# A three-stage kernel (pooled attention and two feed-forward layers): the whole program in written order, weight combination in single steps over three stages

## The chip, the cores and the metric

One core of a Trainium2 chip. The metric is device time in microseconds (us), lower is better: 1559.36 us is the median of three runs before the change (1557.54 to 1560.79). The profiled execution took 1558.88 us, and its span from the first to the last instruction is 1557.0 us. Five engines work beside each other: PE (matmul, with weight loads, PEld), DVE (VectorE), ACT (ScalarE), POOL (GpSimd) and SP (SyncE), which here only issues transfers (DMAs).

## The reference

Attention over 8 batches of 576 tokens (32 packed queries first attend to the keys, then every query attends to the 32 results) gives x of 4608 x 512. Then twice a feed-forward layer with 512 -> 2048 -> 512 columns:

```python
def _moe_ref(x, w_in, w_out):
    h = x @ w_in
    g = h * np.cos(h)
    return (g @ w_out).astype(np.float32)

def _moe2_ref(x, w_in, w_out):
    h = x @ w_in
    g = np.where(h >= 1, h, np.where(h <= -1, 0.0, (h + 1) ** 2 / 4.0))
    return (g @ w_out).astype(np.float32)
```

The weights come as 64-bit floats, so the kernel also has to turn their bits into 32-bit numbers.

## The kernel before

Every float32 matmul is made of three matmuls of float32r parts: a tile is split in a high part (ACT, a copy that rounds) and a low part (source minus high part), and high x high, high x low and low x high are summed in PSUM (`TERMS`). `split` (L68) does one such split.

The program has four stages, and the tokens are transposed: 128 features lie on the partitions, 288 tokens (half a batch, `HB`) in a row.

- **Stage one** (to 353 us): attention and the first layer's up product (`up`, L494), 128 items of 12 matmuls; its result goes to DRAM as `h1T`. In between, `cut_w_out` turns `w_out` into parts.
- **Stage two** (`run_down1`, matmuls L672): 16 blocks of 288 tokens, each of 8 steps of 24 matmuls. Step i needs the argument `r` of step i: load `h`, divide by the turn (`act_a`: ACT L628, DVE L629), sine and product (`act_b`: ACT L636, DVE L637), split (`part`: ACT L69, DVE L70).
- **Stage three** (`run_up2`, matmuls L590): the second layer's up product as a Winograd form of Strassen's scheme: 7 products instead of 8 (X1, Z6, Y5, X2, Z7, Y3, Z4) on sums of quarters of the tokens (`load_y`, on POOL) and of the weights. 8 batches p, 4 column pairs f each, 12 matmuls to a product; PSUM has one bank pair for X, one for Y and two for Z. A product is copied or added to an earlier one (L563, L568), and four of the seven then pass the activation (`activate`: ACT L574, L575, DVE L576) and go to DRAM as `gT`.
- **Stage four** (`run_down2`, matmuls L777): the same scheme for the down product, in groups of 12 matmuls per argument: `load_g` brings quarters of `gT` (called g), `source` makes a difference where needed (DVE L759) and splits it.

The seven sums of the second layer's weights are made in 16 units by `combine` (L419): load 1 MB, scale (ACT), convert (five DVE instructions), four sums, four splits, and store to DRAM (`su` for up, `sd` for down). The 8 up units run in stage two, the 8 down units in stage three. `step("wt")` lets the generator go on by one piece; a piece is a whole conversion, all four sums, or one split.

The order of the work: up to the start of block 1 of stage two, `in_order` chains the instructions of PE, ACT, DVE and SP in the order in which the program writes them. Everything after is ordered by the framework's scheduler, which goes by its own time line, and the pools of stage four are opened when those of stage three are closed.

Of the kernel before, what the change touches and what calls it, by code (L numbers as in the profile page):

```python
# [19 lines left out]
WO_FROM = 36  # L20
WO_SHARE = {0: 1.2, 6: 0.7, 12: 1.3, 13: 1.3, 14: 1.3, 15: 1.3}
# [9 lines left out]
def body(ctx: ExitStack, tc: tile.TileContext, q, k, v, p, w_in, w_out, w_in2, w_out2, out):  # L31
# [387 lines left out]
    def combine(units):  # L419
        def load(src):  # L420
            raw = prep[0].tile([128, 4, 256, 2], I32, tag="raw", name="raw")
            for x in range(2):
                nc.sync.dma_start(out=raw[:, 2 * x:2 * x + 2], in_=src(x))
            return raw

        held = []

        def store():
            for dst, x in held:
                nc.sync.dma_start(out=dst, in_=x)  # L430
            held.clear()

        units = list(units)
        raw = load(units[0][0])
        yield
        for u, (_, dst) in enumerate(units):

            a = prep[0].tile([128, 4, 256], F32, tag="pa", name="pa")
            convert(raw, a, last_act)
            store()  # L440
            yield
            s, hl = (
                raw[:, 2 * i:2 * i + 2].rearrange("p m c t -> p (m c t)") for i in range(2)
            )
            s = s.bitcast(F32).rearrange("p (k c) -> p k c", c=256)
            hls = [hl.bitcast(F32R).rearrange("p (l n c) -> p l n c", l=2, n=2),
                   prep[0].tile([128, 2, 2, 256], F32R, tag="pl", name="pl")]
            tt = nc.vector.tensor_tensor
            tt(out=s[:, 0], in0=a[:, 1], in1=a[:, 3], op=ALU.add)
            tt(out=s[:, 2], in0=a[:, 0], in1=a[:, 1], op=ALU.subtract)  # L450
            tt(out=s[:, 1], in0=s[:, 0], in1=a[:, 0], op=ALU.subtract)
            tt(out=s[:, 3], in0=a[:, 2], in1=s[:, 1], op=ALU.subtract)
            yield
            for j, (k, n) in enumerate(((0, 2), (2, 1), (3, 2), (5, 2))):
                hl = hls[j % 2]
                x = {0: a[:, 0:4:2], 2: a[:, 3:4], 3: s[:, :2], 5: s[:, 2:]}[k]
                with behind(last_act):
                    split(hl[:, 0, :n], hl[:, 1, :n], x, nc.vector)
                for i in range(n):
                    held.append((dst(k + i), hl[:, :, i].bitcast(F32)))  # L460
                yield
                store()
            if u + 1 < len(units):
                raw = load(units[u + 1][0])
                yield

    def units_up():
        for ch in range(2):
            for h in range(2):
                for d in range(2):  # L470
                    def src(x, ch=ch, h=h, d=d):
                        r = w_in2[(d + 2 * x) * 128:(d + 2 * x + 1) * 128, :]
                        r = words(r).rearrange("p (m c t) -> p m c t", m=2, t=2)
                        return r[:, :, ch * 512 + h * 256:ch * 512 + h * 256 + 256]

                    yield src, lambda k, ch=ch, h=h, d=d: su[ch, k][:, d, :, h * 256:h * 256 + 256]

    def units_down():
        for f in range(8):
            yield lambda x, f=f: words(w_out2[(f + 8 * x) * 128:(f + 8 * x + 1) * 128, :]).rearrange(  # L480
                "p (m c t) -> p m c t", m=2, t=2), lambda k, f=f: sd[k, f // 4][:, f % 4]
# [23 lines left out]
    up2 = {}  # L505
# [19 lines left out]
    n_t = [0]  # L525

    def load_y(p):
# [4 lines left out]
        def tile_of(o, src):  # L532
            t = up2[n_t[0] % 8].tile([128, 2, 2, HB], F32R, tag="ty", name="ty")
            n_t[0] += 1
            split(t[:, :, 0], t[:, :, 1], src)
            TY[p, o] = t

        def diff(a, b, x=None):
            if x is None:
                x = up2["d"].tile([128, 2, HB], F32, tag="td", name="td", bufs=2)  # L540
            nc.gpsimd.tensor_tensor(out=x, in0=a, in1=b, op=ALU.subtract)
            return x

        tile_of("X1", b11)
        t1 = diff(b12, b11)
        t2 = diff(b22, t1)
        tile_of("Z6", t2)
        yield
        tile_of("Y5", t1)
        tile_of("X2", b21)  # L550
        tile_of("Z7", diff(b22, b12))
        tile_of("Y3", b22)
        tile_of("Z4", diff(b21, t2, t2))
# [17 lines left out]
    def activate(h, f, t0):  # L571

        t = wtile(up2["o"], "t", 4)
        nc.scalar.activation(out=t, in_=h, func=AF.Relu, scale=0.5, bias=half)  # L574
        nc.scalar.activation(out=t, in_=t, func=AF.Square)  # L575
        nc.vector.scalar_tensor_tensor(out=t, in0=h, scalar=1.0, in1=t, op0=ALU.max, op1=ALU.min)  # L576
        late_store(gT[f // 2, :, t0 // HB], t)
        begin_stores(1)

    def product_up(p, f, o, st):  # L580

# [12 lines left out]
        ta, tb = p * S, p * S + HB  # L594
        if o == "X1":
            st["p1"] = copied(up2["o"], ps, "p1", 2)
        elif o == "Y5":
            st["q"] = added(up2["o"], ps, st["p1"], "q", 2)
        elif o == "X2":
            activate(copied(up2["o"], ps, "hh", 3), f, ta)  # L600
        elif o == "Z6":
            st["u"] = added(up2["o"], ps, st["p1"], "u", 2)
        elif o == "Y3":
            activate(added(up2["o"], ps, st["u"], "hh", 3), f, tb)
        elif o == "Z7":
            activate(added(up2["o"], ps, st["q"], "hh", 3), f + 8, tb)
        else:
            activate(added(up2["o"], ps, st["p1"], "hh", 3), f + 8, ta)

# [14 lines left out]
    def act_a(i):  # L624
        if i < B * 16:
            t = turns[i] = dn1["t"].tile([128, 2, HB], F32, tag="t", name="t")
            ki = t.bitcast(I32)
            nc.scalar.activation(out=ki, in_=G1[i], func=AF.Copy, scale=1 / (2 * PI), bias=0.25)  # L628
            nc.vector.scalar_tensor_tensor(  # L629
                out=t, in0=G1[i], scalar=1 / (2 * PI), in1=ki, op0=ALU.mult, op1=ALU.subtract  # L630
            )

    def act_b(i):
        if i < B * 16:
            t = turns[i]
            nc.scalar.activation(out=t, in_=t, func=AF.Sin, scale=2 * PI, bias=halfpi)  # L636
            nc.vector.tensor_tensor(out=t, in0=G1.pop(i), in1=t, op=ALU.mult)  # L637

    def part(i):
        if i < B * 16:  # L640
            r = parts[i] = dn1["r"].tile([128, 2, 2, HB], F32R, tag="r", name="r1")
            split(r[:, 0], r[:, 1], turns.pop(i), nc.vector)

    def run_down1(w_out_ops, in_order):
        for x in (0, 1, "d"):
            up2[x] = pu.enter_context(tc.tile_pool(name=f"up_{x}", bufs=1, reuse_waits="tile"))
        po = pd.enter_context(tc.tile_pool(name="dn_o", bufs=3, reuse_waits="tile"))
        first_y = None
        prep[:] = [pd.enter_context(tc.tile_pool(name="prep1", bufs=1, reuse_waits="tile"))]
        streams["wt"].append(combine(units_up()))  # L650
        last_act.clear()

        for i in range(B * 16):
# [4 lines left out]
            part(i + 1)  # L658
            act_b(i + 2)
            act_a(i + 3)  # L660
# [4 lines left out]
            if blk == 1 and c == 0:  # L665
                in_order()
            for k in range(2):
                f = 2 * c + k
                for d in range(NDT):
                    ds = slice(d * 128, d * 128 + 128)  # L670
                    for n, (w, y) in enumerate(TERMS):
                        mm = nc.tensor.matmul(  # L672
                            out=acc[d // 2][:, d % 2], lhsT=wo[f // 4, w][:, f % 4, ds], rhs=r[:, y, k],
                            start=f == n == 0, stop=f == NFT - 1 and n == 2, skip_group_check=True,
                        )
            if c == 7:
                for j in range(2):
                    y = po.tile([128, 2, HB], F32, tag="o", name="o1")
                    if j:
                        nc.vector.tensor_copy(out=y, in_=acc[j])  # L680
                    else:
                        nc.scalar.activation(out=y, in_=acc[j], func=AF.Copy)
                    late_store(
                        yT[j * 256:j * 256 + 256, blk * HB:blk * HB + HB].rearrange("(j p) t -> p j t", p=128), y
                    )
            else:
                begin_stores()
            if i % 8 in (1, 3, 4, 6, 7):
                step("wt")
            if i == 13 * 8:  # L690
                drain("wt")
                with tc.issue_after(mm.ins):
                    for o in ORDER_UP[:6]:
                        load_su(0, o)
                first_y = load_y(0)
                next(first_y)
        begin_stores()
        up2["rest"] = first_y
        pd.close()

    def run_up2():
        def pool(name, **kw):
            return pu.enter_context(tc.tile_pool(name="up_" + name, bufs=1, reuse_waits="tile", **kw))

        for i in range(2, 8):
            up2[i] = pool(str(i), side="right")
        up2["o"] = pool("o")
        load_su(0, ORDER_UP[6])
        for _ in up2["rest"]:
            pass  # L710
        for o in ORDER_UP:
            load_su(1, o)
        prep[:] = [pool("prep")]
        streams["wt"].append(combine(units_down()))
        last = None
        for p in range(B):
            for f in range(0, 8, 2):
                if f == 2 and p + 1 < B:
                    for _ in load_y(p + 1):
                        pass  # L720
                st = {}
                for o in ORDER_UP[:6]:
                    product_up(p, f, o, st)
                    if o in ("X1", "X2", "Y5"):
# [367 lines left out]
```

## Time and profile before

| | us |
|---|---|
| median of three runs | 1559.36 |
| profiled execution | 1558.88 |
| its span | 1557.0 |
| PE busy, share of the span | 1491.2, 96% |
| DVE busy | 1178.3, 76% |
| ACT busy | 918.5, 59% |
| POOL busy | 154.4, 10% |

PE is busy nearly all the time, but the busy time of overlapping matmuls says nothing of their pace: a stage has to be compared with its number of matmuls times the distance of two matmuls where nothing waits. A stall is paid twice where the granted clock of PE drops after it.

### The profile page before, as it was taken

Reading aid. Unit: us, or ns where it says so; the run is one execution under the profiler, and the core shown is the slowest. Engines: PE = TensorE matmul, PEld = TensorE weight load, DVE = VectorE, ACT = ScalarE, POOL = GpSimd, SP = SyncE. Lnnn points to the kernel's source line nnn. Section 1 sums busy time; section 2 is a strip of 40 time slices with the busy share of each in tenths; the row PEclk is TensorE's granted clock in tenths of the full one; section 3 lists DMA queues with packets and bytes.
Section 4 is the critical chain, followed back from the end, with each engine's and each line's share of the span. In section 5 each row is a group of like instructions: output and inputs, shape, how many; then the busy total and the mean of one; then the engine's idle time right before and its main releaser. Section 6 shows DMA issues by size and latency. Waiting matters only on the chain. (4 is left out here: it accounts for less than half of the span.)

```text
span 1557.0 us, 29710 instructions
## 1 busy us (share of the span) xinstructions
PE 1491.2 (96%) x11796; PEld 1419.0 (91%) x11796; DVE 1178.3 (76%) x1673; ACT 918.5 (59%) x1424; POOL 154.4 (10%) x94
## 2 busy tenths in 40 slices
PE   8899999999999999999988999999997999999998
PEld 5678788889999999999988999999997999999998
DVE  7784667678898889877468888986665967777874
ACT  4555566567666776766556766766664444444442
POOL 0000000000100000000215423543320000000000
PEclk9799999999999999999998999999999999999999
DMA  9676776466667965634565645653379554444430
GB/s 352 207 241 224 257 258 224 171 240 197 203 196 231 341 193 177 185 108 124 192 230 178 223 166 207 227 185 124 138 279 388 175 153 120 146 126 121 120 109 31
DMA packets 155787, 302.36 MB, mean 194 GB/s; under 512 B 13312, under 2 KB 59392, under 8 KB 152064
## 3 DMA queue, kind: packets, MB, share of 16 engines
q1 hardware_dynamic: 155648, 300.47, 58.0%
q8 instruction: 92, 1.51, 0.4%
q14 instruction: 47, 0.39, 0.1%
HBM read 176.69 MB, written 123.73 MB: 193 GB/s over the span
## 5 line engine op out<-in xcount | busy, mean ns | idle before, releaser
L69 ACT ACTIVATE r<-g 128x576 fp32r<-128x576 f32 x224 | 153.7, 686 | 183.3 <-PE psZ L777 67.2
L494 PEld LDWEIGHTS hps<-at,m 128*128 128x128 f32 x1536 | 208.3, 189 | 46.3 <-ACT u L500 17.9
L494 PE MATMUL hps<-at,m 128*128 128x288 f32 x1536 | 226.1, 302 | 8.7 <-ACT at L322 3.8
L70 DVE TENSOR_TENSOR r<-g,r 128x576 fp32r<-128x576 f32 x224 | 166.3, 754 | 71.6 <-ACT r L69 71.4
L672 PE MATMUL psZ<-r,wo 128*128 128x288 f32 x1536 | 206.6, 296 | 0.0
L672 PEld LDWEIGHTS psZ<-r,wo 128*128 128x128 f32 x1536 | 205.3, 188 | 0.2
L576 DVE SCALAR_TENSOR_TENSOR t<-hh,t 128x576 f32<-128x576 f32 x128 | 120.7, 946 | 31.2 <-ACT t L575 30.9
L500 ACT ACTIVATE u<-hps 128x576 f32<-128x576 f32 x128 | 83.1, 650 | 95.1 <-PE hps L494 58.7
L574 ACT ACTIVATE t<-hh,half 128x576 f32<-128x576 f32 x128 | 98.8, 773 | 64.9 <-DVE hh L568 54.3
L672 PE MATMUL psX<-r,wo 128*128 128x288 f32 x768 | 127.6, 301 | 8.8 <-DVE r L70 8.0
L70 DVE TENSOR_TENSOR r<-t,r 128x576 fp32r<-128x576 f32 x128 | 98.3, 768 | 43.1 <-ACT r L69 42.7
L672 PE MATMUL psY<-r,wo 128*128 128x288 f32 x768 | 125.9, 299 | 0.0
L69 ACT ACTIVATE r<-t 128x576 fp32r<-128x576 f32 x128 | 86.6, 678 | 62.0 <-PE psZ L672 31.8
L672 PEld LDWEIGHTS psX<-r,wo 128*128 128x128 f32 x768 | 111.9, 192 | 10.4 <-DVE r L70 9.2
L672 PEld LDWEIGHTS psY<-r,wo 128*128 128x128 f32 x768 | 111.8, 191 | 0.0
L636 ACT ACTIVATE t<-t,halfpi 128x576 f32<-128x576 f32 x128 | 97.6, 767 | 20.9 <-DVE t L629 20.8
L777 PE MATMUL psZ<-r,so 128*128 128x288 f32 x768 | 105.1, 296 | 0.9 <-DVE o L568 0.9
L777 PE MATMUL psY<-r,sw 128*128 128x288 f32 x768 | 105.6, 296 | 0.1
L777 PEld LDWEIGHTS psZ<-r,so 128*128 128x128 f32 x768 | 103.2, 188 | 1.1 <-issue 1.1
L777 PEld LDWEIGHTS psY<-r,sw 128*128 128x128 f32 x768 | 103.4, 188 | 0.4 <-DVE r L70 0.4
L629 DVE SCALAR_TENSOR_TENSOR t<-h,t 128x576 f32<-128x576 f32 x128 | 97.2, 763 | 7.6 <-ACT t L628 4.2
L759 DVE TENSOR_TENSOR g<-g 128x576 f32<-128x576 f32 x128 | 93.7, 752 | 8.4 <-DMA g<-gT 7.4
(141 smaller groups left out, 2599.6 us busy)
## 6 DMA issues: line engine op xcount, KB each, us to landing
h1T<-u SPq DMA_DIRECT2D x128, 288.0 KB, 3.8
h<-h1T SPq DMA_DIRECT2D x128, 288.0 KB, 3.2
gT<-t SPq DMA_DIRECT2D x128, 288.0 KB, 2.5
g<-gT SPq DMA_DIRECT2D x128, 288.0 KB, 3.2
raw<-in_moe_w_in SPq DMA_DIRECT2D x32, 512.0 KB, 7.6
raw<-in_moe_w_out SPq DMA_DIRECT2D x32, 512.0 KB, 5.3
k<-in_k SPq DMA_DIRECT2D x8, 1152.0 KB, 8.8
yT<-o SPq DMA_DIRECT2D x32, 288.0 KB, 3.5
```

The source lines that it names most:

```text
L69: nc.scalar.activation(out=hi, in_=src, func=AF.Copy)
L70: (eng or nc.gpsimd).tensor_tensor(out=lo, in0=src, in1=hi.bitcast(F32), op=ALU.subtract)
L494: nc.tensor.matmul(out=hps[:, j, :HB], lhsT=m[:, w, G, cs], rhs=x[:, G, y], start=(G == 0 and i == 0), stop=(G == 1 and i == 2),)
L500: last_act[:] = [nc.scalar.activation(out=u, in_=hps[:, :, :HB], func=AF.Copy).ins]
L574: nc.scalar.activation(out=t, in_=h, func=AF.Relu, scale=0.5, bias=half)
L576: nc.vector.scalar_tensor_tensor(out=t, in0=h, scalar=1.0, in1=t, op0=ALU.max, op1=ALU.min)
L629: nc.vector.scalar_tensor_tensor(out=t, in0=G1[i], scalar=1 / (2 * PI), in1=ki, op0=ALU.mult, op1=ALU.subtract)
L636: nc.scalar.activation(out=t, in_=t, func=AF.Sin, scale=2 * PI, bias=halfpi)
L672: mm = nc.tensor.matmul(out=acc[d // 2][:, d % 2], lhsT=wo[f // 4, w][:, f % 4, ds], rhs=r[:, y, k], start=f == n == 0, stop=f == NFT - 1 ...
L759: nc.vector.tensor_tensor(out=b[out], in0=b[x], in1=b[y], op=ALU.subtract)
L777: nc.tensor.matmul(out=ps[:, j], lhsT=s[:, f % 4, w, j * 128:j * 128 + 128], rhs=r[:, y, k], start=first and f == n == 0, stop=f == 7 and ...
```

## The change

The chain of the written order now covers the whole program and POOL too: `in_order()` is called at the end. What the scheduler placed is now placed in the text.

- **Combination** (`combine`): one instruction or two per step, 13 steps a unit; the high part of the last splits is made a step ahead of the low part; the low part overwrites its source; 8 stores a unit, each of one to two sums. The first 2 of the 16 units run in stage one (at items `FIRST_AT` of 16, from item 29 on), 8 in stage two (13 of 15 steps), 6 in stage three (13 of the 28 slots of a batch, `UNIT_AT`).
- **Stage two**: the five parts of the argument are separate (`turn_k`, `turn_t`, `turn_s`, `turn_m`, `part_hi`, `part_lo`) and are written behind the matmuls of step i for steps i+1 to i+4. A block's results are copied in steps 0 and 1 of the next block. The split of the first batch's tokens for stage three runs on DVE in the last nine steps (before: POOL). Weights `su` are loaded at steps `SU_AT`.
- **Stage three**: seven slots per column pair, one product in each; `beside(k, ...)` writes the work that goes beside slot k, one piece of each chain at a time, for the current pair and the one before. The differences of the tokens overwrite the loaded tile (POOL, as before, from the second batch on) and are spread over slots (`Y_AT`). Rings: `t` 6 tiles (before 4), `ty` 9 (before 8), `u` and `q` 1 (before 2).
- **Stage four**: opens no pools of its own apart from one; g lies in the tiles of stage three. The first two quarters are loaded and the weights of three products issued in the last batch of stage three, and four arguments are made there (`ahead`). Arguments run five groups ahead; the low part follows one argument later (`finish_source`).

```diff
+N_FIRST = 2
+UNITS_1 = 8
+UNIT_FROM = 20
+FIRST_AT = (0, 5, 10, 13, 14)
+SU_AT = tuple(range(70, 94, 4)) + (122, 124, 126, 127)
+Y_LOAD = 112
...
     def run_down1(w_out_ops, in_order):
...
             load_h1(i + 7)
-            part(i + 1)
-            act_b(i + 2)
-            act_a(i + 3)
             r = parts.pop(i)
...
-            if blk == 1 and c == 0:
-                in_order()
...
+            part_lo(i + 1)
+            turn_m(i + 2)
+            turn_t(i + 3)
+            turn_k(i + 4)
+            part_hi(i + 2)
+            turn_s(i + 3)
+            begin_stores()
...
-            if i % 8 in (1, 3, 4, 6, 7):
+            if i < UNITS_1 * 15 and i % 15 not in (1, 2):
                 step("wt")
+            if i in SU_AT:
+                load_su(*order[n_su[0]])
+                n_su[0] += 1
+            if i == Y_LOAD or i >= B * 16 - 9:
+                next(ys)
...
+    UNIT_AT = (20, 25, 27, 0, 1, 3, 6, 7, 8, 10, 13, 14, 15)
+    Y_AT = {(2, 2): 3, (2, 6): 2, (6, 2): 1, (6, 4): 2, (6, 6): 1}
...
+                def fill(k):
+                    x = 28 * p + f // 2 * 7 + k
+                    if x >= UNIT_FROM and x % 28 in UNIT_AT:
+                        step("wt")
+                    if p == B - 1 and f == 6 and n_r[0] < 4 and k in (1, 3, 5, 6):
+                        ahead()
+
+                for k, o in enumerate(("X1", "Z4", "Z6", "Y5", "X2", "Z7", "Y3")):
+                    if k != 1:
+                        products_up(p, f, o, cur)
+                    elif old:
+                        products_up(*old["at"], o, old)
...
+                    beside(k, cur, old, fill)
+                    begin_stores(1)
...
+    def beside(k, cur, old, fill):
...
+        elif k == 2:
+            if old:
+                old["h", "Z4"] = added(pool, old["Z"], old["p1"], "hh", 3)
+                select(old, "Z7")
+                square(old, "Y3")
+            fill(2)
+        elif k == 3:
+            if cur:
+                cur["u"] = added(pool, cur["Z"], cur["p1"], "u", 1)
+            if old:
+                relu(old, "Z4")
+                square(old, "Z4")
+            fill(3)
...
+    D2_AT[0, 2] = d2_g0
+    D2_AT[4, 3] = d2_g1
+    D2_AT[4, 0] = lambda: load_sd("X1")
+    D2_AT[4, 2] = lambda: load_sd("Y5")
+    D2_AT[4, 4] = lambda: load_sd("X2")
...
+            if d2_todo:
+                while d2_todo and n_r[0] <= g + 4:
+                    source(*d2_todo.popleft())
+            else:
+                finish_source()
...
-    in_order = ordered(E.PE, E.Activation, E.DVE, E.SP)
+    in_order = ordered(E.PE, E.Activation, E.DVE, E.SP, E.Pool)
...
+    old = run_up2()
+    run_down2(old)
+    in_order()
```

DVE in the middle of stage three, where a unit is worked on. `hh`, `u` and `q` are results of products taken from PSUM, `t` the activation, `raw`, `pa` and `pl` the tiles of a unit. Before:

```order
L568 TENSOR_TENSOR hh<-psZ,p_10754 128x576
L576 SCALAR_TENSOR_TENSOR t<-hh,t 128x576
L568 TENSOR_TENSOR u<-psZ,p_10886 128x576
L449 TENSOR_TENSOR raw<-pa 128x256
L450 TENSOR_TENSOR raw<-pa 128x256
L70 TENSOR_TENSOR raw<-pa,raw 128x512
L568 TENSOR_TENSOR q<-psY,p_10886 128x576
L70 TENSOR_TENSOR pl<-pa,pl 128x256
L451 TENSOR_TENSOR raw<-raw,pa 128x256
L576 SCALAR_TENSOR_TENSOR t<-hh,t 128x576
L452 TENSOR_TENSOR raw<-pa,raw 128x256
L576 SCALAR_TENSOR_TENSOR t<-hh,t 128x576
```

Between two results of products there stood up to three instructions of a unit. At the first slots of a batch after the change:

```order
L597 TENSOR_TENSOR hh<-psY,u 128x576
L146 SCALAR_TENSOR_TENSOR pa<-raw,pa 128x1024
L629 SCALAR_TENSOR_TENSOR t<-hh,t 128x576
L150 TENSOR_SCALAR raw<-pa 128x1024
L597 TENSOR_TENSOR hh<-psZ,p_10419 128x576
L629 SCALAR_TENSOR_TENSOR t<-hh,t 128x576
L597 TENSOR_TENSOR u<-psZ,p_10556 128x576
L152 SCALAR_TENSOR_TENSOR raw<-raw 128x1024
L597 TENSOR_TENSOR q<-psY,p_10556 128x576
```

Here one instruction of a unit at most stands in a slot, and the result of a product comes first in its slot.

SP at the turn from stage three to stage four: `gT` are stores of stage three, `sm`, `sw`, `so` loads of 1 MB of stage four's weights, `g` loads of its quarters. Before:

```order
L88 DMA gT_76<-t_13039 128x576
L513 DMA sw_13310<-sd_75 128x2048
L750 DMA g_13278<-gT_76 128x576
L750 DMA g_13280<-gT_76 128x576
L750 DMA g_13282<-gT_76 128x576
L750 DMA g_13284<-gT_76 128x576
L88 DMA gT_76<-t_13058 128x576
L513 DMA sw_13312<-sd_75 128x2048
L513 DMA so_13314<-sd_75 128x2048
L513 DMA so_13316<-sd_75 128x2048
L513 DMA so_13318<-sd_75 128x2048
L88 DMA gT_76<-t_13077 128x576
```

The third and fourth quarters came behind all weights and the last stores. From the last batch of stage three on, after the change:

```order
L847 DMA g_12743<-gT 128x576 x4
L94 DMA gT<-t 128x576 x6
L531 DMA sm<-sd 128x2048 x2
L94 DMA gT<-t 128x576 x2
L531 DMA sw<-sd 128x2048 x2
L847 DMA g_13016<-gT 128x576 x3
L847 DMA g1b<-gT 128x576
L94 DMA gT<-t 128x576
L531 DMA sw<-sd 128x2048 x2
L94 DMA gT<-t 128x576 x8
L847 DMA g<-gT 128x576 x4
L531 DMA sw<-sd 128x2048 x2
```

The first quarter now stands ahead of the weights, the second behind four of them, the third behind six, and the last eight weights follow between quarters and results.

## Rows read from the trace of the kernel before

**Rows 1.** The page, busy time by engine, and PE's granted clock in 40 slices.

```profile
PE 1491.2 (96%) x11796; PEld 1419.0 (91%) x11796; DVE 1178.3 (76%) x1673; ACT 918.5 (59%) x1424; POOL 154.4 (10%) x94
...
PEclk9799999999999999999998999999999999999999
```

**Rows 2.** Windows of the stages: length, then busy time (instructions) of each engine.

```profile
100.00:340.00 240.00, 235.68 (x2433) 195.70 (x2425) 158.82 (x240) 142.15 (x233) 0.00 (x0) 1.00 0.68 232
...
353.60:777.40 423.80, 415.75 (x3072) 414.22 (x3073) 344.57 (x497) 285.48 (x441) 17.53 (x11) 0.99 0.61 194
777.40:1177.00 399.60, 376.06 (x2675) 370.49 (x2674) 307.37 (x386) 263.09 (x402) 136.16 (x77) 0.96 0.57 202
1177.00:1553.10 376.10, 364.92 (x2705) 363.26 (x2703) 280.68 (x399) 167.96 (x249) 0.00 (x0) 0.99 0.46 143
```

**Rows 3.** The chain that ended last: start, length, matmuls of one product.

```profile
1238.35 6.40 PE psZ L777 x48
```

**Rows 4.** Waits of PE in stage two: total, times, longest.

```profile
PE psX L672 <- DVE r L70: 8.0, 4, 4.9
```

**Rows 5.** Waits of PE in stage three.

```profile
PE psZ L590 <- DVE hh L568: 14.5, 8, 3.6
PE psX L590 <- ACT p L563: 4.9, 3, 2.8
```

**Rows 6.** Waits of PE in stage four.

```profile
PE psX L777 <- ACT r L69: 9.0, 2, 8.1
```

**Rows 7.** Time line of PE in stage two around its longest stall.

```profile
431.85 1.57 PE L672 MATMUL psX<-r,wo 128*128 128x288 f32 x5 [4.86 <-DVE r L70]
433.22 1.64 PE L672 MATMUL psY<-r,wo 128*128 128x288 f32 x6
...
438.57 0.97 PE L672 MATMUL psY<-r,wo 128*128 128x288 f32 x6
```

**Rows 8.** Time line of POOL and DVE ahead of that stall.

```profile
423.04 1.95 POOL L70 TENSOR_TENSOR ty<-yb,ty 128x576 fp32r<-128x576 f32 x1
...
423.62 1.99 DVE L637 TENSOR_TENSOR t<-h,t 128x576 f32<-128x576 f32 x1
```

**Rows 9.** Time line of DVE and PE around the longest stall of stage three.

```profile
832.53 1.95 DVE L576 SCALAR_TENSOR_TENSOR t<-hh,t 128x576 f32<-128x576 f32 x1
834.40 0.74 DVE L568 TENSOR_TENSOR hh<-psZ,q 128x576 f32<-128x576 f32 x1
...
835.20 3.25 PE L590 MATMUL psZ<-ty,so 128*128 128x288 f32 x12 [3.63 <-DVE hh L568]
```

**Rows 10.** Time line of SP and PE at the turn to stage four.

```profile
1191.49 6.59 SPq L88 DMA_DIRECT2D gT<-t  x3
1198.13 13.74 SPq L750 DMA_DIRECT2D g<-gT  x13
...
1202.83 0.61 PE L777 MATMUL psX<-r,sw 128*128 128x288 f32 x1 [8.13 <-ACT r L69]
```

**Rows 11.** DVE by form from 445 to 740 us: count, busy and mean ns.

```profile
L70 DVE TENSOR_TENSOR r<-t,r 128x576 fp32r<-128x576 f32 x93 | 70.1, 753 | 29.8 <-ACT r L69 29.8
...
L146 DVE SCALAR_TENSOR_TENSOR raw<-raw 128x1024 f32<-128x1024 uint32 x6 | 7.3, 1223 | 0.0
...
L70 DVE TENSOR_TENSOR raw<-raw 128x512 fp32r<-128x512 f32 x6 | 4.1, 685 | 0.0
...
L449 DVE TENSOR_TENSOR raw<-pa 128x256 f32<-128x256 f32 x6 | 2.5, 417 | 0.0
```

**Rows 12.** DVE by form from 777 to 1177 us.

```profile
L576 DVE SCALAR_TENSOR_TENSOR t<-hh,t 128x576 f32<-128x576 f32 x122 | 116.3, 955 | 25.9 <-ACT t L575 25.6
...
L146 DVE SCALAR_TENSOR_TENSOR raw<-raw 128x1024 f32<-128x1024 uint32 x8 | 13.4, 1670 | 0.0
```

**Rows 13.** Transfers by line: size, median us from issue to landing.

```profile
yT<-o SPq DMA_DIRECT2D x32, 288.0 KB, 3.5
yb<-yT SPq DMA_DIRECT2D x8, 1152.0 KB, 6.5
```

More of the change, by code (lines that the diff above doesn't have):

```diff
@@ L417, in cut_w_out, with combine @@
         yield 0.75
-    def combine(units):
-        def load(src):
-            raw = prep[0].tile([128, 4, 256, 2], I32, tag="raw", name="raw")
+    def combine(units, tiles):
+        for load, dst in units:
+            raw, a, h1 = tiles()
             for x in range(2):
[L423 to L440, printed above, removed]
+                nc.sync.dma_start(out=raw[:, 2 * x:2 * x + 2], in_=load(x))
             yield
-            s, hl = (
+            scaled(raw)
+            yield
+            yield from converted(raw, a)
+            s, h0 = (
                 raw[:, 2 * i:2 * i + 2].rearrange("p m c t -> p (m c t)") for i in range(2)
@@ L451, in combine @@
             tt(out=s[:, 1], in0=s[:, 0], in1=a[:, 0], op=ALU.subtract)
             tt(out=s[:, 3], in0=a[:, 2], in1=s[:, 1], op=ALU.subtract)
+            high(0)
+            high(1)
             yield
[L454 to L462, printed above, removed]
@@ L463, in combine, with prep_tiles @@
-            if u + 1 < len(units):
-                raw = load(units[u + 1][0])
-                yield
+            low(0)
+            low(1)
+            high(2)
+            high(3)
+            yield
+            low(2)
+            store(0)
+            store(1)
+            yield
+            low(3)
+            store(2)
+            yield
+            store(3)
+            yield
+    def prep_tiles():
+        return (
+            prep[0].tile([128, 4, 256, 2], I32, tag="raw", name="raw"),
+            prep[0].tile([128, 4, 256], F32, tag="pa", name="pa"),
+            prep[0].tile([128, 4, 256], F32R, tag="pl", name="pl"),
+        )
@@ L569, in added, with products_up @@
         return r
[L571 to L580, printed above, removed]
+    def products_up(p, f, o, st):
         x, first = o[0], o in ("X1", "Y5", "Z6")
@@ L716, in run_up2 @@
+        ys, eng, rest = up2.pop("rest")
+        old, n_fill = None, [0]
+        eng[0] = nc.gpsimd
         for p in range(B):
             for f in range(0, 8, 2):
[L718 to L724, printed above, removed]
[L725 to L727 removed]
@@ new lines, in body, with finish_source @@
+    half_done = []
+    def finish_source():
+        if not half_done:
+            return
+        p, o, c, r, src = half_done.pop()
+        nc.vector.tensor_tensor(out=r[:, 1], in0=src, in1=r[:, 0].bitcast(F32), op=ALU.subtract)
+        R[p, o, c] = r
+        if p + 1 < B:
+            if o == "Y3" and c == 0:
+                for i in range(4):
+                    load_g(p + 1, 0, i)
+            elif o == "Z7":
+                load_g(p + 1, 2, c)
+            elif o == "Z4":
+                load_g(p + 1, 1, c)
+                load_g(p + 1, 3, c)
@@ L1038, in body @@
             item()
+            if i > 28 and i % 16 in FIRST_AT:
+                step("first")
             if i == WO_FROM:
```

438 lines of the change are left out of this document (267 added, 171 removed).

## The prediction, made before the result was known

> **What bounds the kernel now.** I read the page first, then the windows of the stages, then who PE waits for in each, and last the time lines around the longest waits. The page has PE busy 96% of the span, DVE 76%, ACT 59%, POOL 10% [rows 1]. That 96% is no proof of a full PE, since it counts slow matmuls as well as fast ones. The pace where nothing waits is on the chain: 48 matmuls in 6.40 us, 0.1333 us each [rows 3]. With it each stage has a floor.
>
> Stage two has 3072 matmuls, 409.6 us; its window is 423.8 us [rows 2], so 14.2 us are lost. Stages three and four have 2688 each, 716.8 us together; their windows are 399.6 and 376.1 us [rows 2], 775.7 us, so 58.9 us are lost. Stage one has mixed shapes and no such floor, but from 100 to 340 us PE is busy 235.7 of 240 us at full clock, with DVE at 158.8 and ACT at 142.2 us [rows 2]: PE bound too, with little to gain. The result leaves in the last 3.9 us. All that a better order can win is about 73 us of 1557.
>
> Where do they go? In stage two PE waits 8.0 us for the low part of its argument, 4.9 us of it at once [rows 4]. After that wait six matmuls take 1.64 us against 0.97 us later [rows 7]: the lower of PE's two clock levels (1.2 instead of 2.4 GHz) for four such rows, 23 matmuls x 0.11 us = 2.5 us more. So a stall is paid about one and a half times. What made it late is ahead of it: POOL splits tokens of stage three there, and a DVE product beside it takes 1.99 us [rows 8] instead of the 0.75 us of its kind [rows 11]. In stage three PE waits 14.5 us for a product's sum on DVE and 4.9 us for a copy on ACT [rows 5], and at 835 us one sees why: DVE had the activation for 1.95 us, then the sum, 0.74 us, and PE stood 3.63 us for it and then ran at half pace, 3.25 us for twelve [rows 9]. In stage four 8.1 of 9.0 us are one wait [rows 6]: SP issued three late stores over 6.6 us and only then the quarters, from 1198.1 us on, while PE stood until 1202.8 us [rows 10].
>
> **The change part by part.** All sums are made against the profiled execution (span 1557.0, time 1558.88, so 1.9 us around it); the median of the runs is 0.5 us above it.
>
> Stage one gets two units. A unit on DVE is thirteen instructions: three of 1.22 us, five of 0.69, five of 0.42 [rows 11] (one row of each length stands there), 9.2 us. Two are 18.4 us. From below: DVE has 81 us free in the 240 us window, so they may cost nothing. From above: every one of the 18.4 us ahead of something PE waits for, and ACT's scalings and high parts queued in front of the copies that free PSUM. One instruction per item is far from the upper end; I take 3 us. What waits behind a late one is the next item's copy or low part, and one item of PE covers it.
>
> Stage two keeps its three DVE instructions per step: 3 x 0.75 = 2.26 us of the 3.2 us that 24 matmuls take. Eight units, 73.6 us, now lie over 120 steps, 0.61 us a step; with the block's copy 0.1 us that is 2.97 of 3.2 us, 93%, less what neighbouring instructions overlap. It fits, but only because nothing else disturbs DVE: the POOL work that doubled its instructions is gone, since the first batch's split goes to DVE in the last nine steps, where no unit runs (one instruction of 0.75 us a step, 3.0 of 3.2 us). The arguments are written two steps ahead, 6.4 us, so a step that runs 1 us over is caught. I leave 2 of the 14.2 us lost, for the first steps; from below 0, from above the 14.2 of now.
>
> Turn to stage three. The first copy of X still lies in memory that stage two's last results leave, so it waits for a store of 3.5 us [rows 13]. PE has three products, 4.8 us, before it needs that copy. Before, the store stood among 1 MB loads; now four of those are issued earlier and four behind it. I take 2 us; 0 to 6.
>
> Stage three itself. Per batch PE has 28 slots of 1.6 us, 44.8 us. DVE has 20 sums of 0.74 us [rows 9] and 16 activations of 0.955 us, and one unit, stretched as its kind is here, 1670 over 1223 ns [rows 11, 12]: 14.8 + 15.3 + 12.6 = 42.7 us, 95%. Starts follow each other closer than the durations say (the sum at 834.40 us starts 1.87 us after an activation of 1.95 us [rows 9]): 0.08 us for each of 49 instructions makes it 38.8 us. On the average PE is the bound. Within a batch it is not even: the first seven slots carry four of the five conversion steps, 5 x 0.74 + 4 x 0.955 + 1.37 x 4.35 = 13.5 us against 11.2; the next seven 12.3. Less the overlap of 30 instructions this is 23.4 us in 22.4. A product's sum has two slots before PE wants the bank again, 3.2 - 0.74 = 2.4 us of lead, and DVE falls behind by 1 to 2.5 us depending on how POOL's steps fall. So PE is just caught, or waits a little in each of seven batches. I take 1 us each, 7 us; from below 0, from above the wait of now (14.5 + 4.9 us [rows 5] times one and a half, 29 us).
>
> Here a rule has to be weighed. Beside POOL a DVE instruction lasted 1.99 us instead of 0.75 [rows 8], while sums from PSUM stay at 0.74 [rows 9]. The Trainium skill (SBUF — State Buffer, section SBUF: two separate sides) says that a DVE instruction with two SBUF inputs and a GpSimd one hold that pair as an exclusive lock, so that the loser waits for the whole other instruction. The trace agrees in size: 1.24 us more is most of POOL's 1.95. By that rule every one of the eleven POOL steps of a batch can cost DVE as much, which is the first rival below.
>
> Turn to stage four and its body. The first two quarters are loaded 26 and 11 slots ahead, 41 and 17 us, four arguments are made before, and the third quarter is wanted only after some 14 us; three late stores no longer stand before it. Of the pair of waits, 9.0 us and their slow matmuls, I leave 1.5. What is late next would be the weights: 14 MB are issued from 22 us before the turn to 21 us after it, each at least 14 us before its first matmul; if they come late PE stands again as at 1202 us. The body already runs at the floor. The last wait for Z, 0.9 us, stays.
>
> Sum: 1557.0 + 3 - 14.2 + 2 - 58.9 + 2 + 7 + 1.5 + 0.9 = 1500.3 us span, 1502.2 us with what lies around it; against the median 1502.7. I say 1502.
>
> **The rivals.**
>
> A. DVE and POOL block each other, and stage three becomes bound by DVE. Per batch: 36 instructions at 0.74 and a unit of 9.2 us are 35.8 us; eleven POOL steps that each add 1.24 us [rows 8] make 49.5 us against PE's 44.8, 4.7 us over. Seven batches: 33 us in place of the 7, so 1502 + 26 = 1528 us. For it: DVE is denser than now and cannot slip past a blocked instruction, as its order is fixed. Against: the stretch now is 0.2 us on the activation on the average [rows 11, 12], and POOL's steps are spread over the slots, at most three in a row.
>
> B. Stage one and two pay for the density: the 18.4 us in stage one go on PE's path, and stage two keeps half its loss. 1502 + 15 + 5 = 1522 us. For it: PE in stage one is at 98%, so lateness of the others has no gap to go into. Against: one instruction per item, and waits of PE in that stage are short.
>
> C, slower: SP. It issues in order and now stands at each batch's token load until POOL has read the old tokens; behind it are the stores of `gT`, and their six tiles are what ACT writes next. The ring gives 4 slots, 6.4 us. Beyond that PE loses what SP stands. It decides at about 15 us: 9 us lost in each of seven batches makes 1502 + 63 = 1565 us. For it: SP took 13.7 us for thirteen transfers at the turn [rows 10], and a token load takes 6.5 us to land [rows 13]. Against: what SP stands for is one split of the old batch, about 0.7 us on ACT and 1.95 us on POOL [rows 8].
>
> D. The order does not do what it says: PE's waits only change place, each with its half pace, and the time is what it was, 1556 to 1562 us. Against: three of the four places lose their cause, not their turn.
>
> **How the numbers follow.** Forecast 0.70 (1488 to 1514 us: the sum with its terms at 0, and at twice their size), A 0.13 (1515 to 1540), B 0.08 (1514 to 1530), C 0.06, D 0.03. The floor under all is 1557.0 - 14.2 - 58.9 + 1.9 = 1485.8 us; the range begins just above it, at 1487, goes to 1530 us and leaves out C, D and the upper part of A. Faster by over 0.2% (3 us, about what a measurement of this kernel can tell) takes in the forecast, A and B: 0.91. Within it D: 0.03. Slower: C, 0.06.
>
> **What would show it.** PE's granted clock without a dip after 60 us; the windows of stage two near 412 us and of three and four together near 730; no wait of PE over 2 us in them; no POOL work in stage two; DVE's sums at 0.75 us, its activations under 1 us. Wrong in a step: waits of PE for a sum in the first fourteen slots of each batch (A), SP standing at the token load with ACT waiting for stores (C), PE waiting for copies in stage one (B). The prediction is wrong as a whole if stage three takes more than 385 us.

## The result and the profile after

The changed kernel takes 1509.9 us, median of four runs (1508.1 to 1511.4), beside 1558.5 us (1551.7 to 1560.8): the ratio is 0.9695, 95% interval 0.9662 to 0.9727. It is faster, inside the range, and 8 us above the 1502 forecast. The profiled span is 1509.6 us.

First the page (busy time by engine; PE's granted clock in 40 slices), beside [rows 1]:

```profile
PE 1470.4 (97%) x11796; PEld 1400.0 (93%) x11796; DVE 1173.9 (78%) x1682; ACT 907.8 (60%) x1424; POOL 139.8 (9%) x85
...
PEclk9899999999999999999999999999999999999999
```

The dip of the clock in the middle is gone. The windows of the stages (length, then busy time and instructions of PE, PEld, DVE, ACT, POOL; granted clock, DMA share, GB/s), beside [rows 2]:

```profile
100.00:340.00 240.00, 231.63 (x2385) 190.90 (x2384) 168.19 (x255) 142.45 (x235) 0.00 (x0) 0.99 0.71 244
364.40:774.10 409.70, 409.70 (x3073) 409.70 (x3074) 343.04 (x506) 275.75 (x437) 0.00 (x0) 1.00 0.62 195
774.10:1142.10 368.00, 362.25 (x2677) 358.92 (x2677) 298.73 (x363) 263.05 (x396) 139.05 (x79) 1.00 0.57 204
1142.10:1505.80 363.70, 359.50 (x2702) 358.56 (x2700) 270.37 (x396) 159.84 (x246) 0.00 (x0) 1.00 0.46 152
```

Stage two lies on its floor of 409.6 us, with no POOL work. Stages three and four take 731.7 us instead of 775.7, 14.9 above their floor. Stage one has become longer: stage two begins at 364.4 us instead of 353.6. PE's waits from 364 us on (total, times, longest), beside [rows 4 to 6]:

```profile
PE psZ L609 <- DVE u L597: 3.7, 6, 0.7
PE psX L951 <- DVE r L867: 2.8, 1, 2.8
PE psX L609 <- ACT hh L592: 2.0, 1, 2.0
PE psX L747 <- ACT u L518: 1.7, 1, 1.7
PE psZ L951 <- DVE hh L597: 0.9, 1, 0.9
```

Instead of waits of up to 8.1 us there are eleven us in all: one short wait in each of six batches of stage three, one at each turn, and 0.9 us for the last Z. What makes the short ones shows on DVE's time line ahead of the first, then POOL's, then PE's:

```profile
822.18 1.79 DVE L146 SCALAR_TENSOR_TENSOR pa<-raw,pa 128x1024 int32<-128x1024 int32 x1
823.89 1.99 DVE L629 SCALAR_TENSOR_TENSOR t<-hh,t 128x576 f32<-128x576 f32 x1
825.80 1.93 DVE L150 TENSOR_SCALAR raw<-pa 128x1024 int32<-128x1024 int32 x1
827.65 0.74 DVE L597 TENSOR_TENSOR hh<-psZ,p 128x576 f32<-128x576 f32 x1
...
828.99 0.75 DVE L597 TENSOR_TENSOR u<-psZ,p 128x576 f32<-128x576 f32 x1
```

```profile
821.00 4.26 POOL L76 TENSOR_TENSOR ty<-yb,ty 128x576 fp32r<-128x576 f32 x2
825.47 1.71 POOL L76 TENSOR_TENSOR ty<-yb,ty 128x576 fp32r<-128x576 f32 x1 [0.21 <-ACT ty L75]
```

```profile
827.41 1.78 PE L609 MATMUL psX<-ty,sw 128*128 128x288 f32 x12
829.79 1.89 PE L609 MATMUL psZ<-ty,sw 128*128 128x288 f32 x12 [0.60 <-DVE u L597]
```

Three DVE instructions beside POOL's splits take 1.8 to 2.0 us each, and `u` ends 0.6 us too late for Z7, which adds to the bank that `u` reads.

### The profile page after: what moved, and what is told of

Its sections match the earlier page's. It is cut to its first block, busy times and chain, and to the rows that moved or that the text cites. A ratio compares the mean times of both kernels' runs of the same rounds, so it can differ in the third digit from the quotient of the medians.

```text
span 1509.6 us, 29648 instructions
## 1 busy us (share of the span) xinstructions
PE 1470.4 (97%) x11796; PEld 1400.0 (93%) x11796; DVE 1173.9 (78%) x1682; ACT 907.8 (60%) x1424; POOL 139.8 (9%) x85
## 4 chain that ended last, share of the span: by engine, by line
PE 82%; DVE 7%; DMA 7%; issue 2%; ACT 2%; SPq 0%; DVEq 0%; ACTq 0%
PE psZ L747 14%; PE psZ L951 10%; PE hps L512 9%; PE psZ L609 8%; PE psX L747 7%; PE psY L747 7%; PE psY L951 6%; PE psX L951 6%; PE psY L609 5%; PE psX L609 5%; DMA h1T<-u 3%; PE psS L275 2%; PE psM L218 2%; DVE t L629 1%; DMA yb<-yT 1%
## 5 line engine op out<-in xcount | busy, mean ns | idle before, releaser
L76 POOL TENSOR_TENSOR ty<-yb,ty 128x576 fp32r<-128x576 f32 x51 | 91.0, 1790 | 960.9 <-ACT ty L75 960.5
L857 ACT ACTIVATE r<-g 128x576 fp32r<-128x576 f32 x147 | 96.8, 681 | 125.5 <-DVE g L854 116.8
L518 ACT ACTIVATE u<-hps 128x576 f32<-128x576 f32 x128 | 83.0, 650 | 95.3 <-PE hps L512 58.1
L747 PE MATMUL psX<-r,wo 128*128 128x288 f32 x768 | 123.3, 296 | 1.7 <-ACT u L518 1.7
L629 DVE SCALAR_TENSOR_TENSOR t<-hh,t 128x576 f32<-128x576 f32 x128 | 114.0, 910 | 4.8 <-ACT t L625 4.8
L867 DVE TENSOR_TENSOR r<-g,r 128x576 fp32r<-128x576 f32 x147 | 107.4, 752 | 7.1 <-ACT r L857 7.1
L951 PEld LDWEIGHTS psZ<-r,so 128*128 128x128 f32 x768 | 102.8, 188 | 1.1 <-ACT r L857 1.1
L710 DVE TENSOR_TENSOR t<-h,t 128x576 f32<-128x576 f32 x128 | 96.2, 751 | 2.1 <-ACT t L705 2.1
```

What stands on the lines that cost most here:

```text
L76: (eng or nc.gpsimd).tensor_tensor(out=lo, in0=src, in1=hi.bitcast(F32), op=ALU.subtract)
L629: nc.vector.scalar_tensor_tensor(out=t, in0=st["h", o], scalar=1.0, in1=t, op0=ALU.max, op1=ALU.min)
L747: nc.tensor.matmul(out=acc[d // 2][:, d % 2], lhsT=wo[f // 4, w][:, f % 4, ds], rhs=r[:, y, k], start=f == n == 0, stop=f == NFT - 1 and n ...
L857: nc.scalar.activation(out=r[:, 0], in_=b[out], func=AF.Copy)
L867: nc.vector.tensor_tensor(out=r[:, 1], in0=src, in1=r[:, 0].bitcast(F32), op=ALU.subtract)
L951: nc.tensor.matmul(out=ps[:, j], lhsT=w_[:, f % 4, w, j * 128:j * 128 + 128], rhs=r[:, y, k], start=first and f == n == 0, stop=f == 7 and ...
```

## The experiments

ACT's 32 copies of m out of PSUM in stage one (L340) serve as marks: copy 11 and copy 31, counted from 0, lie at 155.3 and 342.4 us before (187.1 us between them) and at 157.0 and 352.2 us after (195.2 us). The first unit begins a little ahead of copy 11.

**What makes stage one longer.** In this run the units' work was replaced by loads and stores.

```diff
-        streams["first"] = deque([combine(units[:N_FIRST], lambda: first_tiles)])
+        streams["first"] = deque([carried(units[:N_FIRST], lambda: first_tiles)])
```

> The two units in stage one only load their 1 MB and store (zeros) at the same items; their 26 DVE and 12 ACT instructions are left out, so the output is not the reference's. T1 (the units' DVE and ACT instructions stand ahead of copies that PE waits for): stage two begins at 354 to 356 us instead of 364.4, PE's stalls between 100 and 354 us fall back to those of before (under 1 us each), total 1499 to 1502. T2 (it is their 2 MB of loads and 32 stores, on SP and the DMA queues): stage two begins at 362 to 365, total 1507 to 1510. T3 (clock noise of the first 60 us): 1.3 us of the 10.7 stay whatever is taken out.

Measured: 188.5 us between the marks, 1504.5 us median (ratio 0.9659, 0.9626 to 0.9693), above the total that T1 gave. By these profiles the transfers cost 1.4 us and the units' instructions the rest (in the trace of the changed kernel these are 26 on DVE, 10 on ACT and 16 stores, not the 12 and 32 of the expectation). How much that is varies: the changed kernel has 195.2, seven siblings (runs with the same stage one) 191.2 to 194.0. Three of them began at the lower clock of the last section and have 191.2 to 191.6, four began at the higher one and have 193.5 to 194.0. This run and the next began at the higher one and the kernel before at the lower, so the 1.4 us is not a comparison of like with like. Which engine, the next run asked:

```diff
+            scaled(raw)
...
+            high(0)
+            high(1)
...
+            high(2)
+            high(3)
```

> As the run in which the two units are only carried, but with their ACT instructions (two scalings of 1.11 us, eight high parts) back at their items; the DVE instructions stay out, so the output is not the reference's. From m copy 11 to 31 (counted from 0) of stage one: 188.5 us without both, 191.2 to 195.2 with both, 187.1 before. Theory (ACT's scaling and high parts stand ahead of copies that PE waits for, as the 1.71 us stall behind a scaling of 1.11 us shows): 191 to 194 us. Rival (DVE's 18.4 us do it): 188 to 190 us.

Measured, in one run: 189.3 us. ACT's part is 0.8 us, the theory falls, and the rival holds: most of it, 2 to 6 us, comes with DVE's 26 instructions. That is a difference of runs, 4.2 to 4.7 us against the four siblings that began alike; no run has DVE's part alone. The stall that I had taken as the proof of ACT reads so (ACT, then PE, of the changed kernel):

```profile
243.74 1.11 ACT L137 ACTIVATE unit<-unit 128x1024 f32<-128x1024 f32 x1
244.75 0.59 ACT L264 ACTIVATE e<-psS 128x512 f32<-128x512 f32 x1
245.22 0.26 ACT L265 ACTIVATE e<-psS 64x128 f32<-64x128 f32 x1
```

```profile
245.54 0.66 PE L260 MATMUL psS<-ident,s 128*128 128x128 f32 x4 [1.71 <-ACT e L265]
```

With ACT's part alone the stall of this kind is still there (1.3 us), but so it is, at 0.7 us, without any unit work. A wait that names ACT tells who came last, not who took the time.

**Can the units stand better?**

```diff
-FIRST_AT = (0, 5, 10, 13, 14)
+FIRST_AT = (3, 4, 6, 8, 15)
```

> The two units keep all their work, but their steps stand behind items 3, 4, 6, 8 and 15 of sixteen instead of 0, 5, 10, 13 and 14. T1a (place decides: item 10 stands right ahead of the transposed weights' copies of item 11, item 0 right ahead of the transposes of item 1): the stalls on e (L265) and x (L293) go, stage two begins at 356 to 360, total 1501 to 1506. T1b (the amount decides, 18.4 us on DVE in a stage whose items have no gap): stage two begins at 362 to 366, total 1507 to 1512, with stalls at other places.

Measured: 201.9 us between the marks, 1512.8 us (0.972, 0.9691 to 0.975): worse between the marks, while the intervals of the totals overlap. The second unit's scaling came two items behind its load, and ACT, in its fixed order, stood for the data with all copies behind it:

```profile
245.82 1.10 ACT L137 ACTIVATE unit<-unit 128x1024 f32<-128x1024 f32 x1 [5.97 <-DMA unit<-in_moe_w_in]
```

So the places were tried again with the 26 steps given as item numbers, (31, 36, 38, ..., 104, 111, 115), and the load well ahead of the scaling:

> As the earlier placing behind items 3, 4, 6, 8, 15, but with 5 to 7 items between a unit's load and its scaling, so that ACT does not stand for the data (5.97 us in that run). From the 11th to the 31st m copy of stage one the kernel before took 187.1 us, the changed kernel and its siblings with the same stage one 191.2 to 195.2, the one without the units' work 188.5. T1a (place decides): 188 to 190 us. T1b (amount decides): 191 to 196 us. Total, since the first 150 us vary by 7 us from run to run, 1500 to 1510 by either.

Measured: 197.1 us, 1511.2 us (0.9691, 0.9656 to 0.9725), a little above both ranges, with one wait of 4.3 us for a copy `u` of stage one (L518). Neither placing beat the one of the change; T1a is not borne out, and no better place was found.

**The turns.** Only SP's order is changed.

```diff
-                            load_su(*rest.pop(0)), load_su(*rest.pop(0))
...
+                            while rest:
+                                load_su(*rest.pop(0))
...
+                for i in range(4):
+                    load_g(0, 2, i)
+                load_g(0, 3, 0)
+                load_g(0, 3, 1)
```

> Order of SP's transfers alone: the last four su weights are issued behind the second batch's token load instead of ahead of it; at the turn to stage four the third quarter and half of the fourth are issued ahead of the late stores. Theory (SP's order decides): the stall of 2.0 us at 797 us and that of 2.8 us at 1164.6 us go, with their slow matmuls 6 to 8 us, total 1502 to 1504. Rival (the DMA queues are full there, the transfers land no earlier): the quarters still land near 1163 us, total 1508 to 1511. Second rival: SP then stands for the quarters' tiles with stores behind it, and ACT waits for a free t tile: total 1510 to 1515.

Measured: 1500.2 us (0.9628, 0.9599 to 0.9657), below the forecast, and both waits are gone. Stages three and four take 725.2 us instead of 731.7, so 6.5 us are the turns'; in its profile stage one, which has no edit, is 3.6 us shorter too. SP at the turn to stage four in the changed kernel, then here:

```profile
1132.82 16.40 SPq L94 DMA_DIRECT2D gT<-t  x8
1149.32 2.51 SPq L847 DMA_DIRECT2D g<-gT  x4
...
1153.29 1.41 SPq L847 DMA_DIRECT2D g<-gT  x2
```

```profile
1131.94 5.48 SPq L847 DMA_DIRECT2D g<-gT  x6
1137.61 4.49 SPq L94 DMA_DIRECT2D gT<-t  x3
```

There SP had stood for late results with the quarters behind them; the order of issue was the cause, not the bandwidth. At the turn to stage three it was not SP's standing: the second batch's tokens are issued 3.7 us into the stage in the changed kernel and 3.6 us here. But there the four loads of 1 MB go out just ahead of them, here behind them, and with that the time to landing changes (transfers from 765 to 800 us, after, then here):

```profile
yb<-yT SPq DMA_DIRECT2D x1, 1152.0 KB, 16.5
```

```profile
yb<-yT SPq DMA_DIRECT2D x1, 1152.0 KB, 5.5
```

**The short waits of stage three.** Two runs ask whose they are.

```diff
-    UNIT_AT = (20, 25, 27, 0, 1, 3, 6, 7, 8, 10, 13, 14, 15)
+    UNIT_AT = (20, 25, 27, 0, 3, 6, 7, 8, 10, 13, 14, 15, 17)
```

> The unit's steps in a batch of stage three stand at slots 20, 25, 27, 0, 3, 6, 7, 8, 10, 13, 14, 15, 17 instead of 20, 25, 27, 0, 1, 3, 6, 7, 8, 10, 13, 14, 15: one conversion less ahead of the sum u of slot 3. Theory (DVE's backlog in the first slots): the six stalls of 0.6 us on u (L597) go, 4 to 5 us with their slow matmuls, total 1504 to 1506. Rival (POOL's steps of slots 0 and 2 hold DVE): the six stalls stay at 0.5 us or more, total 1508 to 1511.

Measured: 1498.4 us (0.9619, 0.9594 to 0.9644), below either forecast; the six waits are gone, stage three takes 358.1 us, 9.9 less (windows as above; the turn's wait, 1.0 us here and 2.0 after, is in both):

```profile
769.73:1127.81 358.08, 357.07 (x2679) 356.84 (x2677) 296.48 (x363) 264.43 (x396) 138.86 (x79) 1.00 0.60 210
```

Another 4.3 us by the profile lie ahead of stage two, where this edit does nothing.

The other run takes POOL's work away and leaves the slots:

```diff
+                for l in range(2):
+                    nc.scalar.activation(out=t[:, :, l], in_=src, func=AF.Copy)
```

> From the second batch on the differences of the tokens are left out and both halves of a token tile are plain copies on ACT, so POOL does nothing in stage three and the output is not the reference's. Rival A in small (POOL's accesses hold DVE): the activations on DVE (L629) fall from 910 ns to about 750, the six stalls on u (0.6 us each) vanish, stage three 358 to 361 us, total 1499 to 1503. Other theory (too many steps ahead of u, whoever works beside): the six stalls stay, stage three 366 to 368.

Measured: 1497.6 us (0.9605, 0.9579 to 0.963), just below the forecast, stage three 359.4 us, the six waits gone as well. The activations (groups of DVE by line between 780 and 1140 us; busy us, mean ns), after and here:

```profile
L629 DVE SCALAR_TENSOR_TENSOR t<-hh,t 128x576 f32<-128x576 f32 x124 | 111.0, 915 | 4.8 <-ACT t L625 4.8
```

```profile
L634 DVE SCALAR_TENSOR_TENSOR t<-hh,t 128x576 f32<-128x576 f32 x126 | 92.0, 750 | 5.1 <-ACT t L630 5.1
```

Either cure alone is enough: the waits need POOL's hold on DVE and one conversion too many ahead of `u`. The waits as listed are 3.7 us; siblings with them have stage three at 365.7 to 366.5 us, so without them 6 to 8 us come back. The step between two of them (829.79 and 875.82 us in the trace after) is 46.0 us, against 44.8 for 28 slots: 1.2 us a batch, twice the wait that is named.

**What made the gain.** Three runs undo one thing each. First, the five conversion instructions in one step again, in stages two and three:

```diff
+    def lumped(steps):
+        for n in cycle((1, 1, 0, 5, 0, 0, 0, 1, 1, 1, 1, 1, 1)):
```

> The five conversion instructions of a unit of stages two and three stand in one step again (in stage three at slot 0 of a batch) instead of in five. Theory (a slot has 1.6 us and the sums' lead is 2.4 us): stage two unchanged at 409.7 to 411 us, since its arguments are two steps ahead; in stage three each of six batches waits 2 to 3 us for a sum instead of 0.6, with slow matmuls 12 to 25 us, total 1515 to 1530. Rival (DVE is busy 81% there and catches up): total 1500 to 1510.

Measured: 1532.6 us (0.9834, 0.9794 to 0.9873), above the forecast. Stage two stays at 409.7 us; stage three takes 394.4, nearly what it took before:

```profile
PE psZ L617 <- DVE u L605: 20.9, 6, 3.5
```

```profile
821.59 3.25 PE L617 MATMUL psZ<-ty,sw 128*128 128x288 f32 x12 [3.46 <-DVE u L605]
```

The first row is the sum, the second the first of the six: nearly the same wait and the same half pace (twelve matmuls in 3.25 us) as at 835 us before [rows 9]. Stage three lost 28 us against its siblings' 366, with 17.2 us more of these waits than their 3.7; the granted clock of the stage is 0.96. The group of five took 7.9 us on DVE ahead of that stall, from 810.80 to 818.67 us, more than its length alone, since two of its instructions ran long where POOL splits tokens:

```profile
811.97 2.34 DVE L147 SCALAR_TENSOR_TENSOR pa<-raw,pa 128x1024 int32<-128x1024 int32 x1
815.08 2.33 DVE L153 SCALAR_TENSOR_TENSOR raw<-raw 128x1024 f32<-128x1024 uint32 x1
```

Second, the chain of the written order ends at block 1 of stage two, and the scheduler orders the rest:

```diff
+            if blk == 1 and c == 0:
+                in_order()
...
-    in_order()
```

> The chain of the written order ends at block 1 of stage two, as before the change; single steps, rings, early loads and places in the text stay, and the framework's scheduler orders the rest. Theory (the written order itself gives most of the gain of stages two to four): stage two takes 415 to 425 us instead of 409.7, stages three and four together 745 to 780 instead of 732, total 1530 to 1570. Rival (the smaller pieces, the deeper rings and the early loads give it): total 1505 to 1520.

Measured: 1517.5 us (0.9724, 0.9678 to 0.9769). My theory falls: over 40 of the 49 us stay without the written order, and the intervals of the two kernels overlap. By the profiles the order is worth 10.6 us from stage two on (1155.8 us here, 1145.2 after). One wait at the turn to stage three, which the scheduler's order brings back, and waits for the argument in stage two, where the changed kernel has none:

```profile
795.64 3.19 PE L609 MATMUL psX<-ty,sw 128*128 128x288 f32 x12 [9.16 <-ACT p L592]
```

```profile
PE psZ L747 <- DVE r L720: 4.5, 5, 1.6
PE psX L747 <- DVE r L720: 2.0, 3, 1.0
```

Third, the first batch's split on POOL again, beside stage two:

```diff
-        eng = [nc.vector]
+        eng = [nc.gpsimd]
```

> The first batch's tokens are split on POOL beside the last nine steps of stage two, as before the change, instead of on DVE. Theory (written two steps ahead, the arguments absorb a DVE instruction that POOL delays by 1.24 us): stage two 409.7 to 411 us, total within 3 us of the changed kernel, 1503 to 1512. Rival (POOL beside DVE was what cost stage two its 14 us): stage two 414 to 424, total 1514 to 1525.

Measured: 1503.6 us (0.9636, 0.9612 to 0.9659), stage two 409.7 us. POOL beside DVE costs nothing in these nine steps (from 739 us on), where no unit runs; there arguments written two steps ahead absorb it. It does not clear POOL of the 4.86 us stall of before: that came at 431.9 us behind POOL work beside a unit's splits, a case that no run has. Nor was POOL alone there, since ACT had stood for the same tokens just before (kernel before):

```profile
421.50 0.69 ACT L69 ACTIVATE ty<-yb 128x576 fp32r<-128x576 f32 x1 [2.83 <-DMA yb<-yT]
```

None of the deeper rings, the early loads and the longer lead was undone by itself; their shares stay open.

**The better version**: the turns and the slots together, then with the other items too.

> SP's order at both turns and the unit's new slots in one kernel. Theory (separate causes, gains add): no PE wait over 1 us behind stage two's first, stage three at 358 to 360, stages three and four 718 to 722 (floor 716.8), total 1490 to 1496. Rival (the waits take each other's place): one of the stalls returns, total 1497 to 1502.

Measured: 1490.5 us (0.9572, 0.9531 to 0.9613), five runs. Stages three and four (windows as above) and all of PE's waits from 370 us on:

```profile
766.20:1123.00 356.80, 356.80 (x2678) 356.80 (x2677) 297.73 (x363) 264.54 (x396) 138.61 (x79) 1.00 0.59 210
1123.00:1484.00 361.00, 359.01 (x2699) 358.21 (x2698) 270.13 (x395) 159.98 (x246) 0.00 (x0) 1.00 0.46 154
```

```profile
PE psZ L951 <- DVE hh L597: 0.9, 1, 0.9
PE psY L951 <- DVE r L867: 0.8, 1, 0.8
PE psX L951 <- DVE r L867: 0.2, 1, 0.2
```

The gains add: 13.9 us in these stages, where the turns alone brought 6.5 and the slots alone 7.9, and the two stages stand 1 us above their floor. Against the changed kernel's profile this one is 20.8 us shorter, but 6.5 of that lie ahead of copy 6 of m, where no edit acts.

> The same with the first two units at the items with gaps as well. By T1a total 1486 to 1492, by T1b as without it, 1490 to 1496.

Measured: 1491.9 us (0.9576, 0.9549 to 0.9603), the same as without, with 196.3 us between the marks against 193.8: T1a fails here too.

## Why the prediction was right, and where 8 us came from

The direction and the size were right: the floors of stages two to four were real, and the long waits went. By term of the sum (floor of 356.8 us for the 223 products between the marks of stage three, 360.0 us behind them; the sum is of the profiled execution, which is 1.5 us above the median, so 9.3 us have to be found):

| term | forecast, us | measured, us |
|---|---|---|
| stage one, two units | +3 | +10.7 |
| stage two above its floor | 2 | 0.1 |
| stage three, its turn and body | 2 + 7 | 11.2 |
| stage four, its turn and last wait | 1.5 + 0.9 | 3.7 |
| all | 16.4 | 25.7 |

- **Stage one** is the mis-sized term, 7.7 of the 9.3 us. The step that failed was "one instruction per item is far from the upper end; I take 3 us", and with it "one item of PE covers it". The profile of before had PE busy 235.7 of 240 us [rows 2]; nothing was left for lateness to go into. Of the 10.7 us, 1.7 lie ahead of copy 11; between the marks the changed kernel lost 8.1, its siblings 4.1 to 6.9, and of this, by the runs above, 1.4 are transfers, 0.8 ACT and the rest DVE. This is rival B's first half, at 4 to 8 of its 18.4 us. The 4.0 us between the changed kernel and its lowest sibling sit in two places: copy 15 comes 42.2 us behind copy 11 instead of 39.2, and copies 29 and 30 lie 11.4 us apart instead of 10.0. At the second place ACT stood for a load of `w_out` with the copy `u` behind it, and PE waited 2.1 us for that copy (0.8 in the sibling):

```profile
342.77 0.65 ACT L137 ACTIVATE raw<-raw 128x512 f32<-128x512 f32 x1 [3.65 <-DMA raw<-in_moe_w_out]
```

- **Stage two** came out as argued, even a little better; B's second half did not happen. That it fits "only because nothing else disturbs DVE" is not borne out for the last nine steps: with POOL there the stage stayed at 409.7 us. What does it is in part the fixed lead of two steps: without the fixed order 6.5 us of waits for the argument came back.
- **Stage three**: "waits a little in each of seven batches", at 1 us each, was six times 1.2 us, and in the place named, a sum in the first slots. Only six units run in the stage, so seven was miscounted; that the total comes within half a microsecond (7.4 for 7) is in part luck. Rival A agrees with the trace in kind: 1.99 us for an activation beside POOL, 750 ns on the average without POOL against 915 with it. So does the exclusive lock of the Trainium skill (SBUF — State Buffer, section SBUF: two separate sides). A's price was not its 33 us: taking POOL away brings 6 to 7 us.
- **The turns** were 2 and 1.5 and lost 3.8 and 2.8 us. At the turn to stage three the step named was not the one: the first copy of X waited 1.25 us for its store and PE did not wait for it. PE's 2.0 us were for a later copy, which stood on ACT, in its fixed order, behind a split for which ACT stood 6.9 us, until the second batch's tokens were there:

```profile
776.51 0.65 ACT L592 ACTIVATE p<-psX 128x576 f32<-128x576 f32 x1 [1.25 <-DMA yT<-o]
794.37 0.68 ACT L75 ACTIVATE ty<-yb 128x576 fp32r<-128x576 f32 x1 [6.87 <-DMA yb<-yT]
```

The forecast for the turn to stage four said that late stores "no longer stand before" the third quarter. They did, for 16.4 us on SP, and the fourth quarter came late; behind the difference that waited for it stood, on DVE, the low part that PE needed:

```profile
1163.15 0.76 DVE L854 TENSOR_TENSOR g<-g,g 128x576 f32<-128x576 f32 x1 [5.43 <-DMA g<-gT]
```

Of rival C this is the mechanism, at the turn only; ACT did wait for stores there, but PE did not in the batches.
- **The rest**: DVE's sums at 0.75 us, activations under 1 us on the average, stage three under 385 us, no dip of the clock on the page behind its second slice, all as said. "No wait of PE over 2 us" failed by two, of 2.8 and 2.02 us. The forecast's band was not what it was said to be: with all terms at 0 the sum is 1486, at twice their size 1519, not 1488 and 1514. The result lies in either.

What stays open: why the same instructions of stage one take 191 us between the marks in some runs and 194 in others, with the clock of the first 60 us as the only thing found that goes with it, and which of DVE's instructions PE waits for there.

## What to carry to other kernels

Compare each stage with its matmul count times the distance of two matmuls, and look first at the longest piece that stands in one step on an in-order engine: five instructions put back into one piece, 7.9 us long beside POOL, cost stage three 28 us, while leaving the written order cost 10.6 us in all. Work moved into a stage whose PE is at 98% is not free even one instruction at a time; whether the two units would cost less in a later stage, no run shows. At a turn of stages read SP's queue in order: a store that waits for a late result holds every load behind it (16.4 us here), and a load that is wanted soon should not go out behind large ones (16.5 us to landing against 5.5).

## What the runs showed of the hardware that was not expected

The same instructions ran in the first 60 us at two paces. PE from 20 to 60 us (busy, instructions; granted clock; DMA share, GB/s), after, then in the better version:

```profile
20.00:60.00 40.00, 34.80 (x361) 0.75 0.75 265
```

```profile
20.00:60.00 40.00, 34.84 (x437) 0.96 0.83 290
```

Both were busy 34.8 us, but one did 361 matmuls and the other 437. Copy 6 of m, which lies ahead of every edit, came at 108.4 to 110.3 us in the seven profiles with the lower clock (0.75 to 0.79, the kernel before and the changed one among them) and at 102.8 to 103.6 us in the seven others: 5 to 7 us that no edit made. The changed kernel's mean clock was 0.988 to 0.989 in all four runs, so its median probably holds these microseconds; its sibling with POOL beside stage two began at the higher clock (mean 0.995) and took 1503.6 us.

A stall of PE costs more than its listed length: 17.2 us of waits more lengthened stage three by 28 us, and 3.7 us by 6 to 8. Part of it is the matmuls behind a stall, which the views count as busy.
